# Products of keys and values on the whole array for batches 1 to 3, keys of a half copied to all 128 rows, with a new order of all instructions

## The chip, the cores and the metric

The kernel runs on one core of a Trainium2 chip. The metric is the device time of one execution in microseconds; the lower the better. Three executions of the kernel before took 168.55, 169.35 and 169.62 us (median 169.35). The profiled execution is the first of them: 168.55 us, of which 166.8 us lie between its first and its last instruction (the span), at a granted TensorE clock of 0.997.

In the profile, PE is TensorE's matmuls, PEld its weight loads, DVE is VectorE, ACT is ScalarE, POOL is GpSimd and SP is SyncE, which only issues DMAs here.

## The reference

A gated linear recurrence for 4 batches, 8 heads, 768 positions and 48 channels a head, and behind it an MLP mixer over tokens and channels:

```python
for t in range(S):                       # B, H, S, D = 4, 8, 768, 48
    state = alpha[:, :, t, :, None] * state + einsum('bhd,bhe->bhde', k[:, :, t], v[:, :, t])
    y[:, :, t] = einsum('bhd,bhde->bhe', q[:, :, t], state)
x = y.transpose(0, 2, 1, 3).reshape(B, S, 384)
h = maximum(x.transpose(0, 2, 1) @ w_tok1, 0) @ w_tok2      # 768 -> 256 -> 768
u = x + h.transpose(0, 2, 1)
out = u + maximum(u @ w_ch1, 0) @ w_ch2                     # 384 -> 1536 -> 384
```

## The kernel before

**Tiling.** Each batch is cut into three chunks of 256 positions; n = 3 * batch + chunk runs from 0 to 11. A chunk is loaded as one tile for each of q, k, v and alpha: 128 rows (partitions), two neighbouring positions ("slots", sl) in each row, 8 heads, 48 channels. Rows 0 to 63 hold the first half of the chunk (128 positions), rows 64 to 127 the second (hf = 0 and 1).

**Attention of a chunk.** `ln`, `P`, `lnP`, `cum`, `E`, `IE` make the running products of alpha and their inverses; `kk` and `qq` (L612) scale keys and queries by them into `pkk` and `pkq` in bf16, each head padded from 48 to 64 columns; for n >= 3, `k0a` and `q0r` scale one slot before. `vb` casts the values in place of rows, and `vs0_`, `vs1_` (`vswap`, L674) copy 64 rows of one slot to the other 64 rows, so that `vb[:, hf]` holds all 128 positions of half hf on 128 rows. Keys and queries are transposed on PE (`trk`, `trq`, copied by `evk`, `evq`) for n < 6, and by a transposing DMA on SP's queue (`dk`, `dq`, then the copy `pq`) for n >= 6. `G` makes the products of keys and queries of a half on 48-row, 64-column parts of the array, `mask` cuts them to the causal part, `y` multiplies them with the values, and `ia`, `ib` add the queries times the state. `x` copies the result out.

**State.** `K` (`kmm`, L678) makes the products of keys and values of each half: for each pair of heads j, slot, half and head r of the pair, one product of 64 rows, 64 columns of keys and 48 of values on a 64x64 quarter of the array, 32 of them where the chunk makes two states and 16 for the last chunk of a batch (nst = 1). The result has 192 columns, head r of a pair on rows 64 r. `s` or `sa` (L698, L702) read it twice over (`twice`), once for each head of the pair, and `s`/`sm` multiply by the decay with `amul`, whose factor is exp(-1024) = 0 for the block of the other head. So the state of a pair is a 128 x 96 matrix with two blocks that are zero.

**Mixer of a batch.** `t1`, `ht`, `t2`, `u` are the token MLP; `u` is transposed on PE for batch 0 (`up`, `ut`) and by a transposing DMA for the others (`ux`). `c1` (L765) and `rt` are the first channel layer in 24 groups of three 128x384 products, `c2` (L770) the second in 24 groups of three, `o` (L774) the last sum, `st` the store. `f1_` and `f3_` are one or three products of zeros that keep PE busy in the start; their results are overwritten.

**Order.** Nothing is scheduled at run time. `ORDER` lists every operation with a letter for its engine (t PE, s ACT, v DVE, g POOL, y SP), `BUFS` the buffer of each value; both were found outside the kernel with a planner's costs, which `build` still carries (`dve`, `act`, `pe` and so on) and which have no effect on what is emitted. Each engine works through its own operations in list order; waits come from the data. A DMA is issued by the queue of SP or ACT in its place in that list. One more wait is added by hand: an operation marked `port=True` that goes to DVE or POOL waits for the last marked operation on the other of the two (`shared`, L641), so that marked DVE and POOL operations never run at the same time:

```python
e, last = self.port_turn, self.port_last
if e:
    if last and last[0] != e:
        self.tc.add_manual_dep(i.ins, last[1].ins.name, ...)
    self.port_last = (e, i)
```

Marked are `P`, `k0a`, `q0r`, `kk`, `qq`, `vb`, `vs`, `sm`, `pq` and the casts of the weights (`cw_`).

Of the kernel before, what the change touches and what calls it, by code (L numbers as in the profile page):

```python
# [9 lines left out]
BF16 = mybir.dt.bfloat16  # L10
AF = mybir.ActivationFunctionType
ALU = mybir.AluOpType
# [51 lines left out]
class Plan:  # L64
# [32 lines left out]
NB = 3  # L97
NX = 6
OFF = -1024.0
# [5 lines left out]
    "la": 2, "lf": 2, "E": 2, "IE": 2, "pkq": 2, "pkk": 2, "vb": 3,  # L105
    "tpk": 4, "tpq": 2, "gtm": 2, "tmp": 2, "ss": 5, "x": 12, "ht": 3, "u": 4, "ut": 2, "rt": 22, "o": 3,
# [6 lines left out]
def build(g):  # L113
# [12 lines left out]
    def attention(n):  # L126
# [70 lines left out]
        for hf in range(2):  # L197
# [7 lines left out]
        KO = O("K", {"PE": (276.0 if nst == 2 else 140.0, 420.0)}, 9.5, writes=[kp], reads=[pkk, vb], preds=[kk, vc] + fill("K", kp) + ([prev_s[1]] if prev_s and k > 0 and n > NB else []),  # L205
               emit=lambda e: g.kmm(kp, pkk, vb, nst), mode="G")
        before = prev_s if k > 0 else None
        states = [before]
        for hf in range(nst):
            s_, sp = V("ss"), states[-1]  # L210
            if sp is None:
                so = O(f"s{hf}_", dve(384), 10, writes=[s_], reads=[kp, E], preds=[KO, et],
                       emit=lambda e, s_=s_, hf=hf: g.sfirst(s_, kp, E, hf, wide))
            else:
                t_ = V("tmp")
                ad = O(f"sa{hf}_", dve(384), 10 + hf, writes=[t_], reads=[kp, sp[0]], preds=[KO, sp[1]],
                       emit=lambda e, t_=t_, hf=hf, s0=sp[0]: g.sadd(t_, kp, s0, hf))
                so = O(f"sm{hf}_", either(dve(384), pool_tt(384)), 11 + hf, writes=[s_], reads=[t_, E], port=True,
                       preds=[ad, et], emit=lambda e, s_=s_, t_=t_, hf=hf: g.smul(e, s_, t_, E, hf, wide))
            states.append((s_, so))  # L220
        for hf, st in enumerate(states[:2]):
            yp, x = V("one"), V("x")
            vs = O(f"vs{hf}_", either(dve(384, True), act(384, True), {"POOL": (405.0, 440.0)}), 10, writes=[vb], reads=[vt],
                   port=True, preds=[KO, vc], emit=lambda e, hf=hf: g.vswap(e, vb, vt, hf))
            held = []
            if st:
                held.append(O(f"i{'ab'[hf]}", pe([96] * 4), 13, writes=[yp], reads=[tpq, st[0]], preds=[evq, st[1]],
                              emit=lambda e, hf=hf, st=st, yp=yp: g.inter(yp, tpq, st[0], hf)))
            yo = O(f"y{hf}_", pe([48] * 8), 14, writes=[yp], reads=[gtm, vb],
                   preds=[masks[hf], vs] + held + (fill("y", yp) if hf else []),  # L230
# [110 lines left out]
ld_kt0s ld_at0y ld_vt0s ld_at1y f1_trq0t ld_kt1s ld_qt0y f3_cumw1t ld_qt1y f1_K0t f1_cumw0t f3_cumw0t f1_cumw1t  # L341
f3_trk0t ln0s ld_at2y ld_vt1s cumw0t f3_K0t IE0s f3_trq0t ln1s kk0g ld_at3s ld_kt2y cumw1t E0s Et0s IE1s qq0v trk0t
ldw_wt10y E1s evk0s ld_qt2s Et1s kk1v trq0t ld_kt3y f3_cumw2t vb0v evq0v qq1g K0t f3_trq1t vs0_0s vb1s s0_0v f1_G00t
ld_qt3y G0_0t sa1_0v f1_trq1t f1_trk1t vs1_0g mask0_0v sm1_0g ld_vt2s K1t ln2s trq1t trk1t P3g sa0_1v evq1s f1_G10t
evk1v G1_0t sm0_1g cumw2t mask1_0v ln13s ldw_wt11y f3_G01t Et2s IE2s ld_at4y sa1_1v y0_0t f1_G01t lnP3s f1_y0t G0_1t
kk2v ib0t vs0_1s E2s mask0_1v sm1_1g f3_y1t f1_trk2t y1_0t f1_y1t r13s x0_0s vs1_1g f1_G11t ldw_wt20s x1_0s G1_1t qq2g
ib1t ld_vt3y mask1_1v ia1t cum3t y0_1t E3s trk2t ldw_wt21y vb2s x0_1v ld_qt4y cw_wt10g f1_trq2t evk2v f1_y2t y1_1t
IE3s trq2t k0a3v f1_K2t evq2s f3_K2t kk3v q0r3v t1_0_0_0t K2t t1_0_0_1t f1_G02t sa0_2v G0_2t t1_0_1_0t qq3g t1_0_0_2t
cw_wt11s ldw_wc14y mask0_2v f3_G12t f1_G12t ldw_wc15y vs0_2s x1_1s ldw_wc13y G1_2t P4g vs1_2s ldw_wc11y ld_at5y
t1_0_1_1t mask1_2v t1_0_1_2t ia2t ln14s ldw_wc10y y0_2t t1_0_1_3t trk3t r14s sm0_2v trq3t x0_2s vb3s evk3v t1_0_0_3t  # L350
ib2t y1_2t ldw_wc12y cw_wt21v x1_2s K3t lnP4s cw_wt20g t1_0_1_4t s0_3v t1_0_1_5t ld_kt4y t1_0_0_4t t1_0_0_5t ht_0_1s
cum4t sa1_3v ht_0_0s IE4s sm1_3v t2_0_3t ldw_wc23y vs0_3s t2_0_2t q0r4g u_0_3v E4s t2_0_5t t2_0_4t evq3s u_0_2v
ld_qt5y t2_0_1t cw_wc15g u_0_4v up_0_1t t2_0_0t u_0_5v cw_wc14s qq4g u_0_1v G0_3t u_0_0v ut_0_1s up_0_2t up_0_0t
ut_0_2v ld_kt5s cw_wc13g ut_0_0v trq4t ln15s mask0_3v cw_wc10g evq4s ld_at7y c1_0_10_1t c1_0_7_1t ldw_wc21y P5v
ldw_wc22y c1_0_8_0t cw_wc11v rt_0_7_1s cw_wc12s vs1_3s c1_0_6_1t c1_0_8_1t c1_0_10_0t rt_0_8_0s rt_0_10_1v lnP5s
c1_0_4_0t k0a4g rt_0_6_1v r15s c1_0_1_0t rt_0_10_0v ld_vt4y y0_3t rt_0_4_0v c1_0_0_1t kk4g ldw_wc20y x0_3s cum5t
ld_at6y rt_0_0_1v c1_0_1_1t E5s c1_0_5_1t IE5s rt_0_1_1v cw_wc23g c1_0_9_1t rt_0_1_0v c1_0_7_0t rt_0_8_1v c1_0_6_0t
rt_0_5_1v rt_0_7_0s c1_0_0_0t q0r5v k0a5v rt_0_6_0s G1_3t rt_0_9_1v qq5g c1_0_5_0t ldw_wc25y mask1_3v ldw_wc24y
c1_0_11_1t cw_wc21s ld_kt6y ld_qt6y c1_0_2_1t rt_0_0_0v rt_0_5_0s c1_0_3_0t rt_0_11_1v rt_0_2_1s c1_0_11_0t ld_vt5s
kk5v c1_0_4_1t rt_0_11_0s trq5t vb4s rt_0_3_0v c1_0_2_0t ld_vt6y P7v rt_0_4_1s ld_at9y trk5t rt_0_2_0s cw_wc20g  # L360
c1_0_3_1t evk5v K4t rt_0_3_1s trk4t sa0_4v cw_wc22s ib3t y1_3t c2_0_4_0t c2_0_1_0t sm0_4g vs0_4s x1_3v ln16s ld_qt7s
evk4v vs1_4s ln17s cw_wc25g c1_0_9_0t sa1_4v c2_0_4_1t rt_0_9_0s cw_wc24v G0_4t G1_4t P6g evq5s mask0_4v c2_0_4_2t
c2_0_1_1t sm1_4g c2_0_1_2t mask1_4v ld_kt7y c2_0_1_3t lnP6s ld_at8y k0a6g ld_vt7s c2_0_4_3t o_0_1v vb5s cum6t o_0_4v
ib4t c2_0_2_0t IE6s r17s K5t y1_4t c2_0_5_0t sa0_5v x1_4s G0_5t vs1_5s sm0_5g G1_5t ld_qt8y E6s mask0_5v c2_0_2_1t
# [463 lines left out]
```

## Time and profile before

| | value |
|---|---|
| runs, median | 168.55, 169.35, 169.62 us; 169.35 us |
| profiled execution, and its span | 168.55 us, 166.8 us |
| PE busy, share of span | 158.8 us, 95% |
| c1 (L765) and c2 (L770), 288 products each | 50.7 and 54.2 us |
| DVE, ACT, POOL busy | 118.5, 88.8, 63.9 us |
| read from HBM, written | 25.17 MB, 4.72 MB |
| a load of 384 KB, issue to landing | 4.4 to 10.0 us by kind (medians) |
| transposing DMA of keys, of u | 5.3 us, 3.0 us (medians) |

The DMA engines are busy for nine tenths and more of nearly every slice until 88 us, and for two tenths or less over most of the last 50 us. Times in the profile come from one execution. A matmul's duration in it includes the way through the array, some 0.16 us, which the next one overlaps; the step from one start to the next is what PE is held for.

### The profile page before, as it was taken

Reading aid. Unit: us, or ns where it says so; the run is one execution under the profiler, and the core shown is the slowest. Engines: PE = TensorE matmul, PEld = TensorE weight load, DVE = VectorE, ACT = ScalarE, POOL = GpSimd, SP = SyncE. Lnnn points to the kernel's source line nnn. Section 1 sums busy time; section 2 is a strip of 40 time slices with the busy share of each in tenths; the row PEclk is TensorE's granted clock in tenths of the full one; section 3 lists DMA queues with packets and bytes.
Section 4 is the critical chain, followed back from the end, with each engine's and each line's share of the span. In section 5 each row is a group of like instructions: output and inputs, shape, how many; then the busy total and the mean of one; then the engine's idle time right before and its main releaser. Section 6 shows DMA issues by size and latency. Waiting matters only on the chain.

```text
span 166.8 us, 4619 instructions
## 1 busy us (share of the span) xinstructions
PE 158.8 (95%) x1906; PEld 98.2 (59%) x1906; DVE 118.5 (71%) x208; ACT 88.8 (53%) x170; POOL 63.9 (38%) x68
## 2 busy tenths in 40 slices
PE   7969999889999999999899999999999999999991
PEld 2446565656566676565566676666566665665660
DVE  4059979889898869996998899892588463153522
ACT  3586978988678886735764842428602101641100
POOL 4139476296445661521646739436320000000000
PEclk9999999999999999999999999999999999999998
DMA  5999999999999999899999999489201186200213
GB/s 121 325 325 327 334 356 297 354 363 336 356 367 323 311 325 247 216 251 239 206 200 273 237 271 150 99 212 211 64 0 51 47 68 171 94 0 0 94 51 141
DMA packets 76757, 35.10 MB, mean 210 GB/s; under 512 B 70336, under 2 KB 75712, under 8 KB 76736
## 3 DMA queue, kind: packets, MB, share of 16 engines
q1 hardware_dynamic: 53168, 23.99, 58.5%
q10 hardware_dynamic: 23568, 10.82, 23.4%
q8 instruction: 15, 0.25, 0.7%
q14 instruction: 6, 0.05, 0.1%
HBM read 25.17 MB, written 4.72 MB: 179 GB/s over the span
## 4 chain that ended last, share of the span: by engine, by line
PE 76%; DMA 8%; DVE 6%; ACT 4%; issue 2%; SPq 1%; POOL 1%; DVEq 0%; ACTq 0%
PE ps L770 27%; PE ps L765 25%; PE ps L563 16%; DMA in<-in_q_dram 8%; PE ps L746 3%; PE ps L741 3%; PE ps L624 2%; DVE pkk L612 1%; ACT vb L654 1%; DVE o L774 1%; POOL tpq L655 1%; ACT tpq L654 1%; SPq L504 1%; DVE in L548 1%; DVE in L604 1%
## 5 line engine op out<-in xcount | busy, mean ns | idle before, releaser
L770 PE MATMUL ps<-wc,rt 128*128 128x384 bf16 x288 | 54.2, 326 | 0.1
L765 PE MATMUL ps<-ut,wc 128*128 128x384 bf16 x288 | 50.7, 326 | 0.7 <-DVE o L774 0.7
L736 ACT ACTIVATE rt<-ps 128x384 bf16<-128x384 f32 x52 | 23.5, 491 | 27.8 <-PE ps L765 27.6
L765 PEld LDWEIGHTS <-wc 128*128 128x128 bf16 x288 | 27.2, 98 | 18.4 <-issue 1.2
L770 PEld LDWEIGHTS <-rt 128*128 128x128 bf16 x288 | 26.7, 98 | 16.9 <-issue 0.3
L738 DVE TENSOR_SCALAR rt<-ps 128x384 bf16<-128x384 f32 x44 | 22.8, 551 | 15.5 <-PE ps L765 15.5
L670 DVE TENSOR_TENSOR gtm<-ps,mk 128x1024 bf16<-128x1024 f32 x24 | 28.8, 1220 | 3.6 <-PE ps L563 3.4
L774 DVE TENSOR_TENSOR o<-ps,u 128x384 f32<-128x384 f32 x24 | 13.1, 552 | 7.5 <-PE ps L770 7.4
L612 POOL TENSOR_TENSOR pkq<-in,E 128x768 bf16<-128x768 f32 x7 | 12.7, 1814 | 13.2 <-DVE in L608 7.1
L612 POOL TENSOR_TENSOR pkk<-in,IE 128x768 bf16<-128x768 f32 x7 | 12.7, 1814 | 10.7 <-ACT IE L596 5.2
L563 PE MATMUL ps<-zs 128*128 128x512 bf16 x51 | 15.5, 428 | 1.1 <-DVE zs L468 1.1
L654 ACT CAST vb<-in 64x384 bf16<-64x384 f32 (+1 forms) x24 | 14.5, 603 | 2.7 <-PE ps L563 2.0
L654 ACT CAST x<-ps 128x384 bf16<-128x384 f32 x18 | 8.3, 480 | 13.8 <-PE ps L563 12.6
L750 DVE TENSOR_TENSOR u<-ps,x 128x384 bf16<-128x384 f32 x24 | 12.4, 552 | 3.2 <-PE ps L746 3.1
L707 POOL TENSOR_TENSOR ss<-tmp,E 128x384 bf16<-128x384 f32 x10 | 8.4, 836 | 7.7 <-DVE vb L655 2.4
L703 DVE TENSOR_TENSOR tmp<-ps,ss 128x384 f32<-128x384 f32 x16 | 8.8, 552 | 1.9 <-PE ps L563 1.2
L746 PE MATMUL ps<-ht,wt 128*128 128x384 bf16 x48 | 9.8, 326 | 0.4 <-ACT ht L736 0.4
L612 DVE TENSOR_TENSOR pkq<-in,E 128x768 bf16<-128x768 f32 x5 | 4.8, 953 | 7.2 <-DMA in<-in_q_dram 7.1
L563 PEld LDWEIGHTS <-tpk 48*64 48x64 bf16 x384 | 6.3, 106 | 6.1 <-issue 4.9
L741 PE MATMUL ps<-x,wt 128*128 128x384 bf16 x48 | 9.6, 327 | 0.0
L563 PE MATMUL ps<-tpq,tpk 48*64 48x128 bf16 x384 | 9.1, 220 | 0.4 <-DVE u L750 0.2
L655 POOL COPY tpq<-tpk 128x1024 bf16<-128x1024 bf16 x5 | 6.7, 1339 | 5.8 <-PE ps L770 2.7
(85 smaller groups left out, 191.6 us busy)
## 6 DMA issues: line engine op xcount, KB each, us to landing
in<-in_moe_w_ch_dram SPq DMA_DIRECT2D x12, 384.0 KB, 6.4
in<-in_q_dram SPq DMA_DIRECT2D x10, 384.0 KB, 7.3
in<-in_alpha_dram SPq DMA_DIRECT2D x9, 384.0 KB, 6.5
in<-in_v_dram ACTq DMA_DIRECT2D x9, 384.0 KB, 6.3
in<-in_k_dram ACTq DMA_DIRECT2D x7, 384.0 KB, 5.8
out_dram<-o SPq DMA_DIRECT2D x13, 192.0 KB, 4.2
out_dram<-o ACTq DMA_DIRECT2D x11, 192.0 KB, 1.9
in<-in_k_dram SPq DMA_DIRECT2D x5, 384.0 KB, 6.9
```

Of the source, the lines that this page charges most:

```text
L563: return self.pe.matmul(out, lhsT=lhsT, rhs=rhs, start=start, stop=stop, skip_group_check=True)
L612: self.shared(self.eng[e].tensor_tensor(self.t(dst)[:, :, :, 0:D], self.t(src).rearrange("p h s d -> p s h d"), bass.AP(tensor=f.tensor, o ...
L654: return self.act.copy(d, s)
L670: self.nc.vector.tensor_tensor(self.t(gtm)[:, hf, :, :], self.pair(gp).rearrange("p a (j t) -> p (a j) t", t=128), bass.AP(tensor=m.tensor ...
L736: self.act.activation(d, s, AF.Relu)
L738: self.nc.vector.tensor_scalar_max(d, s, 0.0)
L741: self.pe.matmul(self.bank(bank)[:, 0:HD], lhsT=self.wt1[:, kc, m * 128 : m * 128 + 128], rhs=self.t(x), start=(kc == 0), stop=(kc == NS - 1))
L746: self.pe.matmul(self.bank(bank)[:, 0:HD], lhsT=self.wt2[:, kc, i * 128 : i * 128 + 128], rhs=self.t(hts[kc]), start=(kc == 0), stop=(kc = ...
L750: self.nc.vector.tensor_tensor(self.t(u)[:, i % 3], self.bank(bank)[:, 0:HD], self.t(x), ALU.add)
L765: self.pe.matmul(self.bank(bank)[:, 0:HD], lhsT=self.wc1[:, kc, mc * 128 : mc * 128 + 128], rhs=self.t(ut)[:, 3 * half : 3 * half + 3, kc, ...
L770: self.pe.matmul(self.bank(bank)[:, 0:HD], lhsT=self.t(rts[mc][0])[:, i * 128 : i * 128 + 128], rhs=self.wc2[:, mc, :], start=(mc == 0), s ...
L774: self.nc.vector.tensor_tensor(self.t(o), self.bank(bank)[:, 0:HD], self.t(u)[:, i % 3], ALU.add)
```

## The change

For n >= 3 (`KFN = 3`) `K` is made in another way; for batch 0 it stays as it was.

- `kc` copies the keys of slot 1 of rows 0 to 63 onto rows 64 to 127 of slot 0 in `pkk`, so that `pkk[:, 0]` holds the 128 positions of the first half on 128 rows. Before it, where two states are made (nst = 2), `ka` and `kb` copy rows 64 to 127 of both slots into a new tile `kt`, which then holds the second half. `kc` waits for the transposition of the keys (`trk`, or the landing of `dk`), since it writes over them, and for `ka`.
- `kfull` multiplies 128 rows, 128 columns of keys (two heads) and 96 of values: four products a half, eight or four a chunk. It reads `vb` after `vs`; before, `vs` waited for `K`.
- The result has 384 columns and holds the blocks of the other head too; `sfirst` and `sadd` read it as it is (`kparts`), and the zeros of `amul` still take those blocks away.
- `ka`, `kb`, `kc` may run on DVE, ACT or POOL and are marked for the shared port. In the new order the 21 of them are 12 on ACT, 7 on POOL, 2 on DVE.
- Buffers: E 2 to 3, pkk 2 to 3, ss 5 to 4, kt 1, x 12 to 9, rt 22 to 20.
- `ORDER` and `BUFS` are replaced as a whole: other places, other engines for many operations, other queues for many loads.

The core of the diff:

```diff
+KFN = 3
...
+        vsw = lambda hf, preds: shift(f"vs{hf}_", 10, [vb], [vt], preds, lambda e: g.vswap(e, vb, vt, hf))
+        turned = n >= KFN
+        if turned:
+            vs = [vsw(hf, [vc]) for hf in range(2)]
+            kx, kp_in = None, [kk, vc, vs[0]]
+            if nst == 2:
+                kx = V("kt")
+                ka = shift("ka", 9, [kx], [pkk], [kk], lambda e: g.kturn(e, kx, pkk, 0))
+                kb = shift("kb", 9, [kx], [pkk], [kk], lambda e: g.kturn(e, kx, pkk, 1))
+                kp_in += [ka, kb, vs[1]]
+            kc = shift("kc", 9, [pkk], [], [kk, trk if n < NX else evk] + ([ka] if nst == 2 else []),
+                       lambda e: g.kturn(e, None, pkk, 2))
+            KO = O("K", pe([96] * (4 * nst)), 9.5, writes=[kp], reads=[pkk, vb] + ([kx] if kx else []),
+                   preds=kp_in + [kc] + ([prev_s[1]] if prev_s and k > 0 and n > NB else []),
+                   emit=lambda e: g.kfull(kp, pkk, kx, vb, nst))
...
+    def kturn(self, e, kx, pkk, part):
+        k = self.t(pkk)
+        d, s = ((self.t(kx)[0:64] if kx else None, k[64:128, 0]), (self.t(kx)[64:128] if kx else None, k[64:128, 1]),
+                (k[64:128, 0], k[0:64, 1]))[part]
+        self.copy(e, d[:, :, 0:D], s[:, :, 0:D])
+
+    def kfull(self, kp, pkk, kx, vb, nst):
+        vv = self.t(vb)
+        for hf in range(nst):
+            kk = self.t(kx) if hf else self.t(pkk)[:, 0]
+            for j in range(4):
+                self.mm(self.bank(kp, hf)[:, 96 * j : 96 * j + 96], kk[:, 2 * j : 2 * j + 2, :],
+                        vv[:, hf, 2 * j : 2 * j + 2, :], j == 0, j == 3)
...
+    def kparts(self, kp, hf, turned):
+        b = self.bank(kp, hf)
+        return self.st(b[:, 0:HD]) if turned else self.twice(b[:, 0:192])
```

The new order around the places that matter for batch 1 and 2 (engine letters at the end of each name):

```diff
+ORDER = """
+ld_qt0s ld_at0y ld_kt0s ld_at1y f1_trk0t ld_kt1s ld_vt0y f1_cumw0t f1_cumw1t f1_trq2t f1_trq1t f3_cumw0t ld_vt1y ln0s
+ld_qt1y f3_trq0t f3_cumw1t ld_at2s cumw0t f3_trk0t IE0s f1_trq0t ld_kt2y f3_trq2t Et0s ln1s kk0v E0s cumw1t qq0v trk0t
...
+c2_0_0_0t x0_5s qq6v c2_0_0_1t ln18s k0a6v x1_5s IE7s c2_0_0_2t c2_0_2_2t E7s P9v t1_1_0t IE6s ld_qt8s kk6v c2_0_0_3t
+vb7s t1_1_1t o_0_0v dk6y r18s ht_1_0v vs1_7g c2_0_3_0t c2_0_2_3t kk7g o_0_1v ht_1_1s lnP9s t2_1_3t ld_kt9s t2_1_4t
+ka6s u_1_3v t2_1_5t P11g c2_0_3_1t u_1_4v t2_1_0t u_1_5v cum9t vs1_6g u_1_0v ux_1_1y c2_0_5_0t k0a8g o_0_2v c2_0_5_1t
+t2_1_1t q0r8g st_0_0y t2_1_2t u_1_1v kc6s c2_0_3_2t st_0_1y u_1_2v kb6s vs0_6g c2_0_3_3t ln19s ux_1_0y vb8v c2_0_5_2t
+IE9s P8v K6t lnP11s c2_0_5_3t k0a9v E9s dk7y s0_6v lnP8s kk9g c1_1_0_1t ka7s sa1_6v c1_1_10_1t vs0_7s o_0_3v dq6y
+rt_1_0_1s c1_1_8_1t rt_1_10_1v ld_qt9s c1_1_6_1t sm1_6v kb7s c1_1_2_1t c1_1_3_1t vs1_8s o_0_5v rt_1_8_1s q0r7g r19s
+c1_1_7_1t rt_1_6_1v qq7g rt_1_3_1s c1_1_11_1t rt_1_2_1v rt_1_7_1s cum8t ld_at10y c1_1_1_1t IE8s c1_1_4_1t E8s kc7g
+dq7y c1_1_10_0t rt_1_11_1s kk8g rt_1_1_1s c1_1_5_1t rt_1_4_1s K7t rt_1_10_0s rt_1_5_1v ld_vt9y sa0_7v c1_1_5_0t sm0_7v
...
+"""
```

## The prediction

> **What bounds the kernel now.** I read the page's busy times and 40 slices first, then who waited for whom on PE, then the chain of waits, then PE's timeline stage by stage, then the groups by shape for the price of one instruction.
>
> ```profile
> PE 158.8 (95%) x1906; PEld 98.2 (59%) x1906; DVE 118.5 (71%) x208; ACT 88.8 (53%) x170; POOL 63.9 (38%) x68
> ...
> PE   7969999889999999999899999999999999999991
> ...
> DVE  4059979889898869996998899892588463153522
> ```
>
> PE is full in nearly every slice; DVE stands at 8 or 9 tenths up to about 100 us and falls off after. The next view is PE's waits (total us, times, longest):
>
> ```profile
> PE ps L563 <- DVE zs L468: 1.1, 1, 1.1
> PE ps L624 <- DVE pkq L612: 0.8, 1, 0.8
> PE ps L765 <- DVE o L774: 0.7, 1, 0.7
> PE ps L563 <- ACT vb L654: 0.4, 1, 0.4
> PE ps L746 <- ACT ht L736: 0.4, 1, 0.4
> ```
>
> After 38 us only the 0.7 is left. The chain of waits gives the two marks I work with:
>
> ```profile
> 37.88 4.06 PE ps L765 x24
> ...
> 158.03 5.38 PE ps L770 x33
> 163.41 0.02 issue
> 163.43 0.56 DVE o L774
> ```
>
> From the first channel product (c1, L765) at 37.88 to 163.4 PE is the path; before it the path runs through loads, DVE, ACT and POOL; after it 3.4 us go to the last sum and store. So the span is a start of 37.9, PE's work of 125.5, and 3.4: 166.8. The profiled run took 168.55, 1.75 more, and is the fastest of three with median 169.35, so I scale by 1.0047 at the end.
>
> **The products of keys and values on PE.** PE's timeline (start, us, what):
>
> ```profile
> 50.44 0.65 PE L765 MATMUL ps<-ut,wc 128*128 128x384 bf16 x3
> 51.02 0.44 PE L563 MATMUL ps<-vb,pkk 64*64 64x48 bf16 x32
> 51.39 0.62 PE L624 MATMUL ps<-idn,pkk 128*128 128x128 bf16 x8
> ...
> 95.54 0.42 PE L563 MATMUL ps<-tpq,tpk 48*64 48x128 bf16 x16
> 95.79 0.42 PE L563 MATMUL ps<-vb,pkk 64*64 64x48 bf16 x32
> 96.04 0.43 PE L563 MATMUL ps<-tpq,tpk 48*64 48x128 bf16 x16
> ```
>
> Three L765 products take 0.49, so they give PE free at 50.93; the group K4 holds it until 51.39: 0.46. Between score products (G), which also use part of the array, K9 takes 95.79 to 96.04: 0.25. Coming from and going back to the whole array thus costs about 0.2 a time. The new products have the shape of the state products, 128x96 on the whole array: eight of them start at 61.90 and the next instruction at 62.24, so 0.34 for eight, 0.17 for four. In batches 1 to 3 that is 6 x 0.34 + 3 x 0.17 = 2.55, against 9 x 0.25 = 2.25 plus the switches. In the old order there are 25 stretches of part-array work, 14 of them after the first c1; in the new one 21 and 11.
>
> The Trainium skill (TensorEngine Tiling (Array Packing), When to Use Tiling) says that a contraction or a free dimension of 64 and less is where splitting the array pays; by this alone the change would lose 0.3 us, 2.55 against 2.25, and the row inside G bears it out. The Trainium skill (same page, Key Properties) also says that a change of mode drains the array; the trace agrees, with the 0.2 of a K group by itself.
>
> After the first c1 I add up both orders with the steps of this timeline (c1 and c2 groups 0.49, t1 0.98, t2 0.33, G 0.25, y 0.20, state products 0.17, cum 0.29): old 121.4 + 14 x 0.2 = 124.2, so the old 125.5 hold 1.3 of standing; new 121.0 + 11 x 0.2 = 123.2. The first terms fall by 0.4: the K groups of n = 4 to 11 give 2.21 in the place of 2.0, and two groups move ahead of the first c1 (cum5 0.29, G1_3 0.25). The rest is three stretches fewer, 0.6. **PE after the mark: -1.0.** Ahead of it the order has 54 warming products (L563, 512 wide, 0.21 warm) in the place of 51: 0.6, at nothing, because PE waits there for the other engines anyway; without that cover it is 0.6.
>
> **The copies.** 21 come in: kc 9, ka 6, kb 6. The trace has no bf16 to bf16 copy of 64x384; the nearest rows are the casts of that size:
>
> ```profile
> L654 ACT CAST vb<-in 64x384 bf16<-64x384 f32 x17 | 8.7, 510 | 2.7 <-PE ps L563 2.0 <-issue 0.4
> ...
> L655 POOL CAST vb<-in 64x384 bf16<-64x384 f32 x5 | 2.5, 501 | 7.2 <-DVE ss L707 4.0 <-DVE in L604 3.0
> ...
> L655 DVE CAST vb<-in 64x384 bf16<-64x384 f32 x2 | 0.7, 356 | 0.1
> ```
>
> 12 on ACT are 6.1 us, 7 on POOL 3.5, 2 on DVE 0.7; I take these, with half of them as the lower bound and the 128x768 casts (0.83 on ACT and POOL, 0.55 on DVE) as the upper. The Trainium skill (VectorE: DVE Perf Modes, Mode 4x_2P) lets a copy between two 16-bit tiles in SBUF run at four elements a cycle; an estimate from it is 0.1 us plus a fixed part for each of the two DVE copies, 0.4 less on DVE and nothing in the sum, and no run here shows it. ACT has 27.6 us of waiting for c1 alone in this trace and hides its share; on POOL the copies stand in the chain of the shared port.
>
> **The new order on the other engines.** I count the instructions of both order lists by engine and multiply by the mean durations in the groups by shape. POOL gets kk 7 to 10, qq 7 to 9, k0a 4 to 6, q0r 3 to 6, vs 5 to 9, loses weight casts 8 to 5: 63.0 to 77.6 us. DVE 127.0 to 122.8 in durations (118.5 busy, since neighbours overlap by a tenth), ACT 97.9 to 103.8. The marked DVE and POOL instructions wait for each other in order: this chain grows from 88.1 to 96.7 us, over some 115 us, from 8 to 123. It isn't full, and I price it only in the start and where PE waits for it (below). Before, the half copies of v (vs) waited for K, which read v in place; now K waits for them, and they may go ahead of it. The buffers cut for the new tiles (x 12 to 9, rt 22 to 20, ss 5 to 4) I take at nothing: six x of a batch are read by u (68 to 71 us in batch 1) before the next batch writes its first (90), and the c2 of a batch are nearly done when c1 of the next begins (73.7); if a writer did wait, one c2 group, 0.5, is what it waits for.
>
> **The start.** Old: DVE first waits for q until 10.19, t2 starts at 32.65, first c1 at 37.88. New: q and k of n = 0 are the first loads on ACT, kk0 goes to DVE at 7.9 (where POOL began it before), qq0 at 9.5, vb0 ends at 10.9. Then the shared chain binds, by steps of the timelines (POOL 1.76 for kk and qq, 0.95 for 384 wide, 0.79 for sm, 0.78 for casts, 0.48 for halves; DVE 0.47, 0.87 for 768, 1.13 for masks): kk1, vb1, qq1 to 15.4; sm1_0 16.0; kk2 17.9; sm0_1, vs1_0, P3 to 19.8; sa1_1 and qq2 21.1; sm1_1, k0a3, kk3 24.8; P4, cw_wt21, q0r3 26.3. Now DVE binds: sa0_2, two masks to 29.0, x0_2, x0_1, vb3, x1_2 to 30.9. The last t1 products end at 31.3, K3 and ht bring t2 at 32.3, six sums u run to 36.0, two ut copies to 37.1; on POOL qq4 and the casts of wc14 and wc15 end at 37.2. First c1 at 37.4: -0.5. Bounds: DVE has 31.5 instead of 27.9 queued ahead of the first c1 (3.3 with the overlap), starts 2.3 sooner, so 38.9 if it has no slack; ACT has 1.7 less queued, so 36.3.
>
> **Standing after the mark.** The 0.73 at 79.2 goes: DVE stood for a q load there (q0r9) that SP sent late; q0r7 to q0r9 now run on POOL and ACT sends q7 to q9. What is late next is K6. It stands in PE's queue between c2 groups and now needs vs0_6 and kc6. vs0_6 is on POOL behind kk7, P11, vs1_6, k0a8, q0r8, and q0r8 needs a q load (7.3 us to landing); PE has 8.6 us of work listed from that load to K6 (nine c2 groups, two t1, six t2, cum9), against 7.3 + 1.0 + 0.5 + 0.1: 0.3 late. kc6 waits, on ACT, for the transposing DMA that still reads these keys:
>
> ```profile
> tpk<-pkk SPq DMA_TRANSPOSE x6, 5.3
> ```
>
> 7.1 us of PE's work against 5.3 + 0.5 + 0.1: in time; with the longest landing of that tile, 6.2, too. kb6, ln19, IE9 and lnP11 queue behind kc6 on ACT. K7 after kc7 on POOL (kk8 behind it): 6.2 of work against 5.9, or 6.8 at the longest: 0 to 0.6. The first c1 of batch 1 has 3.9 us behind the transposing DMA of u, which takes 3.0 to 4.8: 0 to 0.9. I take 0.9 for the three, so 1.3 - 0.73 + 0.9 = 1.5; bounds 0.6 and 4.
>
> **Sum:** 37.4 + 123.2 + 1.5 + 3.4 = 165.5 span, 167.25 for this run, 168.0 by the median: 0.8% faster.
>
> **The rivals.** *Faster by over 1%*: start at the lower bound, no new standing: 36.3 + 123.2 + 0.6 + 3.4 = 163.5, 166.0 by the median. For it: DVE is relieved up to 100 us. Against: the shared chain fills the start. *Slower*: K6 waits for the q load behind POOL's queue. If that load lands after 10.0 us (the slowest kind in the page, a weight) instead of 7.3, K6 is 3.0 late, and K7, behind the same POOL queue, 1.5 more; with the start at 38.9: 38.9 + 123.2 + 5.1 + 3.4 = 170.6, 173.2 by the median. It decides above some 4.5 us of standing in all, delay of the start included. For it: DMA is 9 tenths busy until 88 us. Against: ACT sends the load unblocked. *It does not do what it says*: three of nine K groups lay inside G, where only 0.25 could be saved; if the other six switch as often as before, 0.6 goes and the result is 168.6, no change.
>
> **Numbers.** About 1% is what a measurement of this kernel tells from no change: 167.7 to 171.0. Forecast, with the third rival, 0.37; faster 0.34; slower 0.29. The range 165.8 to 172.2 leaves out the ends of both rivals; the likeliest case alone is 167.0 to 169.5.
>
> **What would show it.** 128x96 products of vb in the place of 64x48, 0.34 for eight; the first L765 near 37.4; no wait for o before L765; PE waits before the K groups n = 6 and 7 under 1 us in sum. A PE wait there of 2 us or more, or a first c1 after 39, makes me wrong.

## The result, and the profile after

The changed kernel takes 169.28 us (median of 20 runs, 168.96 to 171.6). The kernel before, run 20 times too, takes 169.2 us (167.48 to 170.81). The ratio of after to before, which leaves out runs more than 1.5% above the fastest of their kernel, is 1.0053, with a 95% interval of 1.0031 to 1.0076: slower by 0.3 to 0.8%, inside the 1% that the prediction takes as no change. The medians of all 20 differ by 0.05%. The forecast was 168.0, faster by 0.8%.

From the page of the changed kernel, busy times and slices:

```profile
PE 158.8 (95%) x1729; PEld 98.9 (59%) x1729; DVE 115.4 (69%) x205; ACT 95.2 (57%) x180; POOL 78.5 (47%) x84
...
PE   7898997989999999999999999999999999999991
...
DVE  4096989999797997878477998887287161663232
...
POOL 4037565798839720958898976884200000000000
```

PE is busy for the same 158.8 us with 177 products fewer in the trace. POOL has 14.6 us more (77.6 were worked out), DVE 3.1 less. PE's thin place behind the first slices is the seventh, 25.1 to 29.3 us; before it had 9 there. PE's waits (total us, times, longest):

```profile
PE ps L588 <- ACT la L582: 1.4, 3, 0.8
PE ps L588 <- DVE zs L491: 1.1, 1, 1.1
PE ps L588 <- DVE tmp L745: 0.9, 1, 0.9
PE ps L787 <- ACT ht L777: 0.4, 1, 0.4
PE ps L782 <- ACT wt L679: 0.3, 1, 0.3
PE ps L588 <- POOL pkk L680: 0.2, 1, 0.2
...
```

The first five are in the start; the wait for o at 79.2 is gone, and the last one shown (before K7) is the only one listed after the first c1. The chain of waits (start, us, what) gives the marks; c1 is L806 now, c2 L811, t1 L782:

```profile
5.76 8.65 DMA in<-in_q_dram
14.57 1.82 POOL pkq L637
17.11 1.83 POOL pkk L637
...
32.24 1.32 PE ps L782 x8
35.31 1.03 DVE u L791 x2
39.43 3.52 PE ps L806 x21
...
154.97 8.79 PE ps L811 x54
163.75 0.02 issue
163.78 0.56 DVE o L815
```

The first c1 starts at 39.36 (the chain's piece begins where the product before it ends, at 39.43), PE ends at 163.74, the span is 167.2. So start, PE's part and tail are 39.36 + 124.4 + 3.4, against 37.88 + 125.5 + 3.4 before and 37.4 + 124.7 + 3.4 in the forecast (123.2 and the 1.5 of standing taken together). The start grew by 1.5; it was to fall by 0.5. PE's part fell by 1.1, where 0.8 was forecast. Here it is by itself, before and after (from:to, length, us; busy us of PE, PEld, DVE, ACT, POOL; granted clock; DMA):

```profile
37.88:163.40 125.52, 124.59 (x1398) 77.99 (x1398) 91.24 (x155) 60.67 (x124) 43.16 (x39) 1.00 0.77 182
39.36:163.74 124.38, 124.05 (x1227) 77.81 (x1220) 84.98 (x144) 67.42 (x135) 55.54 (x53) 1.00 0.73 179
```

PE was busy for 0.5 less and stood for 0.3 in the place of 0.9.

The K groups in PE's timeline (start, us, what), n = 4:

```profile
50.19 0.61 PE L649 MATMUL ps<-idn,pkk 128*128 128x128 bf16 x8
50.63 0.33 PE L588 MATMUL ps<-vb,pkk 128*128 128x96 bf16 x4
50.80 0.33 PE L588 MATMUL ps<-vb,kt 128*128 128x96 bf16 x4
50.97 1.25 PE L806 MATMUL ps<-ut,wc 128*128 128x384 bf16 x6
```

From 50.63 to 50.97 are 0.34 for eight products, and c1 follows at once: nothing of the 0.2 at each side is left. The new copies, by shape (count, busy us, mean ns, idle before):

```profile
L680 DVE COPY pkk<-pkk 64x384 bf16<-64x384 bf16 x2 | 0.5, 253 | 0.1
L679 ACT COPY kt<-pkk 64x384 bf16<-64x384 bf16 x10 | 5.1, 509 | 0.5 <-POOL pkk L637 0.3
L679 ACT COPY pkk<-pkk 64x384 bf16<-64x384 bf16 x2 | 1.0, 509 | 1.0 <-DMA tpk<-pkk 0.9
L680 POOL COPY pkk<-pkk 64x384 bf16<-64x384 bf16 x5 | 2.5, 498 | 0.3
L680 POOL COPY kt<-pkk 64x384 bf16<-64x384 bf16 x2 | 1.0, 500 | 0.1
```

They cost what the casts of that size cost on ACT and POOL, and 253 ns in the place of 356 on DVE. The Trainium skill (VectorE: DVE Perf Modes, Mode 4x_2P) states four elements a cycle for two ports with two packed bf16 each; that the copy is faster than the cast agrees with it, and the rate itself no run here shows.

### The profile page after: what moved, and what is told of

Read it like the earlier page. It is cut to its first block, busy times and chain, and to the rows that moved or that the text cites. A ratio compares the mean times of both kernels' runs of the same rounds, so it can differ in the third digit from the quotient of the medians.

```text
span 167.2 us, 4293 instructions
## 1 busy us (share of the span) xinstructions
PE 158.8 (95%) x1729; PEld 98.9 (59%) x1729; DVE 115.4 (69%) x205; ACT 95.2 (57%) x180; POOL 78.5 (47%) x84
## 4 chain that ended last, share of the span: by engine, by line
PE 76%; DMA 5%; POOL 5%; DVE 4%; ACT 4%; SPq 3%; issue 1%; POOLq 0%; DVEq 0%
PE ps L811 28%; PE ps L806 25%; PE ps L588 11%; DMA in<-in_q_dram 5%; PE ps L782 5%; PE ps L787 4%; SPq L529 3%; POOL pkk L637 2%; POOL pkq L637 2%; PE ps L649 1%; ACT vb L679 1%; ACT tpq L679 1%; DVE ss L748 1%; PE ps L798 1%; DVE gtm L695 1%
## 5 line engine op out<-in xcount | busy, mean ns | idle before, releaser
L811 PE MATMUL ps<-wc,rt 128*128 128x384 bf16 x288 | 53.0, 326 | 0.0
L806 PE MATMUL ps<-ut,wc 128*128 128x384 bf16 x288 | 50.4, 326 | 0.1
L777 ACT ACTIVATE rt<-ps 128x384 bf16<-128x384 f32 x54 | 24.6, 492 | 26.9 <-PE ps L806 26.7
L806 PEld LDWEIGHTS <-wc 128*128 128x128 bf16 x288 | 27.4, 98 | 17.9 <-issue 0.5
L811 PEld LDWEIGHTS <-rt 128*128 128x128 bf16 x288 | 27.0, 98 | 17.0 <-issue 0.2
L779 DVE TENSOR_SCALAR rt<-ps 128x384 bf16<-128x384 f32 x42 | 22.1, 553 | 14.3 <-PE ps L806 14.0
L637 POOL TENSOR_TENSOR pkk<-in,IE 128x768 bf16<-128x768 f32 x10 | 18.2, 1817 | 12.9 <-DVE vb L680 8.5
L637 POOL TENSOR_TENSOR pkq<-in,E 128x768 bf16<-128x768 f32 x9 | 16.3, 1818 | 3.8 <-DVE in L633 1.7
L680 POOL CAST vb<-in 64x384 bf16<-64x384 f32 (+1 forms) x12 | 7.0, 582 | 11.4 <-ACT lf L585 4.9
L679 ACT CAST vb<-in 64x384 bf16<-64x384 f32 (+1 forms) x19 | 11.3, 597 | 0.4
L679 ACT CAST x<-ps 128x384 bf16<-128x384 f32 x13 | 6.1, 479 | 8.7 <-PE ps L588 8.4
L782 PE MATMUL ps<-x,wt 128*128 128x384 bf16 x48 | 9.3, 326 | 0.3 <-ACT wt L679 0.3
L748 POOL TENSOR_TENSOR ss<-tmp,E 128x384 bf16<-128x384 f32 x9 | 7.5, 836 | 3.9 <-DVE pkq L637 2.2
L588 PEld LDWEIGHTS <-zs 128*128 128x128 bf16 x54 | 5.1, 103 | 5.8 <-issue 1.9
```

The source lines that it names most:

```text
L588: return self.pe.matmul(out, lhsT=lhsT, rhs=rhs, start=start, stop=stop, skip_group_check=True)
L637: self.shared(self.eng[e].tensor_tensor(self.t(dst)[:, :, :, 0:D], self.t(src).rearrange("p h s d -> p s h d"), bass.AP(tensor=f.tensor, o ...
L679: return self.act.copy(d, s)
L777: self.act.activation(d, s, AF.Relu)
L779: self.nc.vector.tensor_scalar_max(d, s, 0.0)
L782: self.pe.matmul(self.bank(bank)[:, 0:HD], lhsT=self.wt1[:, kc, m * 128 : m * 128 + 128], rhs=self.t(x), start=(kc == 0), stop=(kc == NS - 1))
```

## The experiments

They ask two things: whether the gain on PE comes from the products, and what holds the start. In the diffs the letters behind a name are the engine; order lists are cut to the places that change. PE's part is always first c1 to PE's end.

### The products

**Old K in the new order.** vs goes back behind K, as the old products need it.

```diff
-KFN = 3
+KFN = 12
...
-ib3t ka4s y1_3t ... rt_0_8_1s kb4s x1_3s ... c1_0_5_1t kc4v vs1_4s ... vs0_4g r15s
+ib3t y1_3t ... rt_0_8_1s x1_3s ... c1_0_5_1t ... r15s ... K4t vs1_4s vs0_4g
...
```

> The new order with the old products of keys and values everywhere (KFN = 12): the 21 copies are gone, vs stands behind K. If the new products are worth on PE what the timelines say (after the first c1 five groups of 0.46 for 0.34 and three of 0.46 for 0.17): PE's part from the first c1 is 1.5 longer than 124.4. Theory A: the first c1 is 1.0 to 1.5 earlier than 39.36 as the copies leave ACT; the span is then within 0.5 of 167.2. Theory L: the first c1 stays near 39.2 and the span is 168.4 to 168.7. Rival for the products (the copies cost as much after the mark as the products save): PE's part stays at 124.4.

174.94 us, ratio 1.0322 (1.0268 to 1.0375). PE's part is 127.9, 3.5 more, of which 2.3 are waits:

```profile
PE ps L805 <- DVE tmp L744: 0.9, 1, 0.9
PE ps L587 <- ACT vb L678: 0.6, 1, 0.6
PE ps L587 <- ACT x L678: 0.5, 1, 0.5
PE ps L805 <- DMA ut<-u: 0.3, 1, 0.3
```

PE is busy for 125.52 of these 127.9, 1.5 more than in after: that is the groups themselves with their switches, as expected. The other 2.1 are standing, and they are the larger share; only the wait for vb is by its row a wait for vs, which stands behind K here, and that the others follow from it isn't shown. The Trainium skill (TensorEngine Tiling (Array Packing), When to Use Tiling) gives a contraction or a free dimension of 64 and less as the case for splitting the array. Inside other part-array work a group of small products is the cheaper one in this kernel, too, 0.25 (K9 of before) against 0.34 (K4 of after); between products on the whole array, at 0.46 (K4 of before), it is not. First c1 is at 42.0: the clock fell to half from 29.7 to 33.1 (below), so nothing is read from this start.

**The old start, then the new order.** All of the list of before up to the first c1, then that of after; buffers are assigned anew where the two lists meet.

```diff
-ld_qt0s ld_at0y ld_kt0s ... t1_0_0_0t ... G1_3t ut_0_2s
+ld_kt0s ld_at0y ld_vt0s ... t1_0_0_0t ... trq4t evq4s
 c1_0_10_0t ...
```

> The order of the kernel before up to its first c1, then the order of the changed kernel for all that is left; n = 3 the old way, n = 4 to 11 the new way. If the start alone is what the change loses and the rest what it gains: first c1 at 37.9, from there to PE's end 124.4 as in the changed kernel plus 0.5 for two groups that the changed kernel had made before its first c1, span 166.2 to 166.4: 0.5% under the changed kernel and 0.3% under the kernel before. Rival (the rest is short only because its start left more vector work done): PE's part grows to 125.5 or more and the span is 167 or more.

171.31 us, 1.0143 (1.01 to 1.0185). First c1 38.76, PE's part 128.4: 2.8 of waits in it (1.1 for rt, 1.0 for E, 0.7 for the q copy), and from the first c1 to the first c2 17.5 in the place of 13.6. The old start leaves work undone that the new one has behind it, five operations of n = 3 and 5 among it (G1_3, cum5, lnP5, E5, IE5). So the rival came true: PE's part of the new order is short only behind the new start. How much of this comes from the reassigned buffers isn't told apart.

**The old order with the new products alone**, n = 4 to 6 and 8 to 11:

```diff
-        turned = n >= KFN
+        turned = n in (4, 5, 6, 8, 9, 10, 11)
...
-K4t trk4t sa0_4v ... sm0_4g vs0_4s x1_3v evk4v vs1_4s
+kb4s ka4s vs0_4s ... vs1_4s ... trk4t kc4s ... K4t sa0_4v ... sm0_4g x1_3v evk4v
...
```

> The order of before in every stage, with one part of the change alone: n = 4, 5, 6, 8, 9, 10 and 11 make K from 128x96 products and copies (ka, kb on ACT, kc on ACT or POOL); their vs stand ahead of K, K itself up to 4 us of PE work later where kc has to wait for the transposition; n = 3 and 7 as before. The start is that of before, so first c1 at 37.9. Theory P (the products themselves are worth what was worked out, 0.1 to 0.3 for a group that stands alone, nothing inside G): PE's part from there 124.8 in the place of 125.5, span 166.1, ratio 0.996. Rival W (the added wait for vs and kc takes the gain back): PE waits before a K group of over 0.5 in sum, span 166.8 or more, ratio 1.000 to 1.005.

175.07 us, 1.037 (1.0322 to 1.0418). First c1 37.6 as in before, PE's part 132.3. PE's waits from there:

```profile
PE ps L785 <- DVE tmp L743: 1.1, 1, 1.1
PE ps L586 <- DVE tmp L743: 1.1, 2, 0.6
PE ps L647 <- ACT rt L775: 1.0, 1, 1.0
PE ps L586 <- DVE o L813: 1.0, 1, 1.0
...
```

Theory P falls, and W as well as it was put: only 0.2 of waiting stands directly before a K group. But ka, kb and vs of n = 4 lie together on ACT from 49.75 to 51.3, and the rt behind them stops PE for 1.0 at 51.9; after that DVE is late again and again up to 131 us. The added copies and waits do take the gain back, through the queues of ACT and DVE and at many times the price. It shows this placing of the copies, put in by hand, not that none would do.

So the new products save PE work, and in these runs the saving reached the time of PE's part only with the new order from the first instruction on. In the changed kernel and the fourteen experiments with its order after the first c1 that follow, PE's part stays between 124.4 and 124.8 whatever the start does. The total moves with the first c1 alone.

### The start: loads

The walk in the prediction against the trace of after: kk2 17.9 at its end, measured 18.9; sa0_2 26.3, measured 27.5; masks of n = 2 done 29.0, 30.3; x1_2 done 30.9, 32.6; t2 32.3, 34.4; first c1 37.4, 39.36. One microsecond is lost by kk2, and one more in steps from there to t2.

**The q load of n = 1 ahead of v.** POOL's qq1 stood for it until 14.57, and DVE 1.30 behind that.

```diff
-f3_cumw0t ld_vt1y ln0s ld_qt1y f3_trq0t
+f3_cumw0t ld_qt1y ld_vt1y ln0s f3_trq0t
...
-s0_0v vb1g f1_G00t ... vs0_0s mask0_0v
+s0_0v f1_G00t ... vs0_0s vb1s mask0_0v
```

> The changed kernel with the load of q for n = 1 sent before that of v for n = 1 on SP's queue, and the cast of that v (vb1) taken from POOL to ACT, where there is a gap after vs0_0. Theory L (the start is late because POOL's qq1 stood for its load until 14.57 us and the shared chain of DVE and POOL carried that delay): qq1 starts at about 13.0, kk2 0.6 to 0.7 earlier than 17.11, the first c1 0.7 earlier (38.7 instead of 39.36), the span 166.5. Theory A (ACT's queue sets the end of the start): the first c1 stays within 0.2 of 39.36.

169.58 us, 1.0034 (1.0002 to 1.0067); first c1 39.50. qq1 began at 13.32, but then the next loads came last, first k of n = 2 (kk2 stood 1.97 until 17.10), then its q. The first c1 came no sooner, as theory A had it. The chain:

```profile
13.07 8.18 DMA in<-in_q_dram
21.25 0.02 issue
21.27 0.96 DVE pkq L637
```

One load alone is not it: all of them are on their way at once, at 325 GB/s, and what is brought forward pushes back its neighbour. A run below (f5_dve_clock) shows by accident what a late load does. There the k load of n = 2 took 9.88:

```profile
8.01 9.88 DMA in<-in_k_dram
...
18.05 1.81 POOL pkk L645
```

kk2 began 0.94 later than in after, ACT's cast of wt10 0.84 later, and the first c1 0.85 later (40.21).

### The start: one engine at a time

**The copies of n = 3 gone** (old K for n = 3: 1.0 us off ACT, 0.5 off POOL).

```diff
-KFN = 3
+KFN = 4
...
-t1_0_1_0t kb3s trq3t x0_1v ka3g lnP4s ... cum4t vs1_3g kc3s x1_2v ... vs0_3s
+t1_0_1_0t trq3t x0_1v lnP4s ... cum4t x1_2v ... E4s vs0_3s ... qq4g vs1_3g
```

> The changed kernel with n = 3 made the old way (KFN = 4): the three copies ka3, kb3, kc3 are gone and vs0_3, vs1_3 stand behind K3. On ACT that takes 1.0 us of copies and 0.5 of vs0_3 from ahead of ht. Theory A (ACT's queue sets the end of the start, and the copies of the change are a part of it): t2 and the first c1 1.0 to 1.5 earlier, span 165.7 to 166.2. Theory L (the late load and the shared chain): the first c1 earlier by 0.3 at most, span 167.0 or more.

170.13 us, 1.0049 (1.0014 to 1.0084); first c1 39.33, the same. The copies alone do not hold the start.

**ACT's queue reordered:** vs0_2 and the cast of wt10 ahead of evk3, cum4 and IE4 behind t1.

```diff
-evk3s ... vs0_2s G1_2t ia2t cw_wt10s ... vb3v cw_wt11s ... cum4t ... IE4s ... ht_0_0s
+vs0_2s cw_wt10s G0_2t ... evk3s ... cw_wt11s kb3s ... cum4t K3t ... ht_0_0s IE4s
```

> The changed kernel with ACT's queue put in another order between 26.7 and 34 us: vs0_2 and the cast of the first token weight (cw_wt10) ahead of evk3, cw_wt11 ahead of kb3, and cum4 and IE4 behind the t1 products and ht. Theory Q (the start is late because the t1 products stand behind ACT's cast at 30.07 and PE then works off 2.0 us of queue before the last eight of them): t1 starts at 29.3 to 29.5, t2 0.4 to 0.8 earlier than 34.39, the first c1 at 38.6 to 39.0. Theory D (DVE's queue sets the end of the start, by the masks that end at 30.2): t2 within 0.2 of 34.39.

170.4 us, 1.0081 (1.004 to 1.0122). In the profiled run the first t1 product began at 30.21, no sooner than in after: it now waits 0.38 for evk3, whose PSUM bank it takes. t2 and the first c1 (39.12) came 0.24 earlier, between what Q and D expected. The clock averaged 0.99 in 8 of its 12 runs, 168.5 to 169.3 of span against 166.8 to 167.4 in the other four, so the median is one with the lower clock.

**DVE's queue reordered** (G0_1 ahead of y1_1; P4 and the cast of wt21 behind vb3 and x1_2), **both**, and **both with u's way shortened** (ut_0_0 on ACT, sa1_3 behind u):

```diff
-evk2v y1_1t ... G0_1t ... P4v trk3t cw_wt21v ... vb3v cw_wt11s ... x1_2v
+evk2v G0_1t y1_1t ... trk3t ... vb3v P4v lnP4s cw_wt11s ... x1_2v cw_wt21v
```

> The changed kernel with DVE's queue relieved between 23 and 31 us: P4 and the cast cw_wt21 go behind vb3 and x1_2, and PE makes G0_1 ahead of y1_1, so that mask0_1 needn't wait 0.64. Theory D: the last mask of n = 2 ends at 28.7 instead of 30.2, t2 1.0 to 1.6 earlier than 34.39. Theory Q: the t1 products still wait for ACT's cast at 30.07, t2 within 0.3 of 34.39.

> Both edits. If the start is held by both queues together: t2 at 32.6 to 33.0, the first c1 at 37.7 to 38.2, the span 165.7 to 166.3, so 0.3 to 0.6% under the kernel before. Rival L (the loads hold the start, whatever the queues do): first c1 above 39.

> Both edits, and the first copy of the transposed u (ut_0_0) on ACT, with sa1_3 behind the six sums u on DVE: 0.5 to 0.8 less on DVE between t2 and the first c1. If DVE's queue holds that last stage: first c1 at 37.0 to 37.6, span 165.2 to 165.8, 0.6 to 1.0% under the kernel before. Rival (POOL's casts of wc14 and wc15, which end at 38.37 in the changed kernel, hold it): first c1 at 38.0 or later, no better than with the two edits alone.

171.38, 170.52 and 171.05 us (1.0187, 1.0134 and 1.0163, all above 1.008 at the lower end); first c1 41.6, 40.6 and 42.7. None shows the gain it was made for; the rivals of the second and third (first c1 above 39; at 38.0 or later) come true by the number, but not by their cause. G0_1 shares its banks with trk2, so PE waited 0.6 to 0.9 there for evk2 and 0.57 more behind it for x; in the first it then waited 1.1 for vb, in the other two 0.9 for evk3. How much of the later c1 each wait makes isn't told apart. In the third the clock fell, too.

**Work taken off one engine, every queue as it was.** Some operations are done for one head of eight, and the rest of them is left out: P4, q0r3, vb3 on DVE; vb2, vs1_2, vs0_2 on ACT; vs1_0, k0a3 on POOL.

```diff
+CUT = ["P4", "q0r3", "vb3"]
...
-        a = self.t(at)
+        a = self.t(at)[:, 0 : self.heads]
...
+            g.heads = 1 if o.name in CUT else 8
             o.emit(o.on)
```

> The changed kernel with three operations of the start that run on DVE ahead of the last t1 products (P4, q0r3, vb3) done for one head of eight: some 1.3 us less work on DVE, every queue as it was. It leaves out part of these products and of one cast. Theory D (DVE is the path of the start: 28 us of work between 8.7 and 39.1 with 2.5 of gaps): first c1 1.0 to 1.3 earlier, 38.0 to 38.4. Theory A (ACT's queue paces it): 0 to 0.3 earlier. Theory L (the loads pace it): 0 to 0.3 earlier, DVE standing longer instead.

> The changed kernel with three casts of the start that run on ACT (vb2, vs1_2, vs0_2) done for one head of eight: some 1.2 us less work on ACT between 24.6 and 29.2. It leaves out the rest of these casts. Theory A: t1 products begin 0.8 to 1.2 earlier and first c1 too, 38.2 to 38.6. Theories D and L: first c1 within 0.3 of 39.36, though t1 begins earlier.

> The changed kernel with two operations of the start that run on POOL in the shared chain (vs1_0, k0a3) done for one head of eight: some 1.2 us less on POOL. It leaves out the rest of them. Theory S (POOL's share of the shared chain holds DVE up): first c1 0.6 to 1.2 earlier. Theories A, D and L: within 0.3 of 39.36.

First c1 40.79, 39.10 and 39.35. POOL is out (theory S falls), ACT gives 0.26 of 1.2 taken away (theory A falls). With less work on DVE it came 1.4 later, with the granted clock at half for a time (from:to, length, us; busy us of PE, PEld, DVE, ACT, POOL; granted clock; DMA):

```profile
28.00:29.00 1.00, 0.66 (x21) 0.51 (x21) 1.00 (x2) 0.99 (x3) 1.00 (x2) 1.00 1.15 370
29.00:30.00 1.00, 0.48 (x13) 0.48 (x13) 0.86 (x1) 0.98 (x2) 0.94 (x3) 0.74 1.10 341
30.00:31.00 1.00, 0.94 (x11) 0.47 (x9) 0.96 (x3) 0.95 (x3) 0.39 (x1) 0.50 1.12 345
31.00:32.00 1.00, 1.00 (x10) 1.00 (x9) 0.17 (x2) 1.00 (x2) 0.68 (x2) 0.50 1.08 398
```

The granted clock, ahead of the last two numbers, is 0.50 from 29.4 to 32.8. So the run says nothing of DVE. It was made again with three warming products into a free bank ahead of y0_2, to keep PE from standing:

```diff
+            if o.name == "y0_2":
+                g.fill2(2, 3)
             o.emit(o.on)
```

> f1_dve_less again (P4, q0r3 and vb3 for one head of eight, the rest of them left out), with three more warming products ahead of the y product that waits from 28.65 to 29.52, so that PE does not stand there and its granted clock should stay at 1.0 (in f1_dve_less it was 0.50 from 29.4 to 32.8). Theory D (DVE is the path of the start): first c1 at 38.0 to 38.4. Theory Q (from the first t1 product on, PE's own queue is the path, so less work on DVE gains nothing): first c1 39.0 to 39.5. If the clock falls again, no verdict on either.

The clock stayed. With the k load 0.94 late, the first t1 product and the first c1 (40.21) are both 0.85 late: of the 1 us taken off DVE 0.1 came through at most in this execution. DVE stood 1.22 for PE ahead of x1_2 instead, and the first t1 product still waited 0.30 for ACT's cast. Theory D falls, as far as one execution with a late load can tell. The same on PE, eight of the twelve t1 products 96 columns wide:

```diff
+        w = 96 if self.early and 0 < kc < NS - 1 else HD
-        self.pe.matmul(self.bank(bank)[:, 0:HD], ..., rhs=self.t(x),
+        self.pe.matmul(self.bank(bank)[:, 0:w], ..., rhs=self.t(x)[:, 0:w],
```

> The changed kernel with eight of the twelve t1 products of batch 0 made 96 columns wide in the place of 384: some 0.8 us less work for PE between 30.1 and 33.6, every queue as it was. It leaves out the rest of these products. Theory Q: first c1 0.5 to 0.8 earlier, 38.6 to 38.9. Theory D: within 0.2 of 39.36. If the clock falls, no verdict.

First c1 40.36, with the clock at 0.50 from 29.4 to 32.8: no verdict on PE.

### The start: several queues together

In after, PE has this before t2 (timeline, start, us, what, the wait before it):

```profile
29.25 0.56 PE L588 MATMUL ps<-vb,gtm 128*128 128x48 bf16 x16 [0.17 <-ACT vb L679]
30.11 0.50 PE L782 MATMUL ps<-x,wt 128*128 128x384 bf16 x2 [0.30 <-ACT wt L679]
...
32.10 1.46 PE L782 MATMUL ps<-x,wt 128*128 128x384 bf16 x8
...
34.39 1.78 PE L787 MATMUL ps<-ht,wt 128*128 128x384 bf16 x10 [0.40 <-ACT ht L777]
```

All twelve t1 products come after 30.11, when the last mask is nearly done. In before the first ran at 24.89, and when its last mask of n = 2 was done, at 29.33, these five were left:

```profile
29.75 0.33 PE L741 MATMUL ps<-x,wt 128*128 128x384 bf16 x1
31.20 0.82 PE L741 MATMUL ps<-x,wt 128*128 128x384 bf16 x4
```

PE works off a queue after that the walk did not have.

**PE's queue mended:**

```diff
-ldw_wt20y ... ldw_wt10y ... cw_wt20s ... trk3t cw_wt21v ... cw_wt10s
+ldw_wt10y ... ldw_wt20y ... cw_wt10s ... trk3t y0_1t t1_0_0_0t cw_wt21v ... cw_wt20s
...
-y0_2t ... y0_1t x0_2v t1_0_0_0t ... t1_0_1_0t ... trq3t x0_1v t1_0_0_1t f1_y2t vb3v ib2t y1_2t ... x1_2v
+y0_2t t1_0_0_1t t1_0_1_0t ... ib2t y1_2t ... x0_1v x0_2v ... trq3t ... x1_2v vb3v
```

> The whole computation, in the order of the changed kernel with PE's queue of the start mended: the loads and casts of wt10 and wt20 change places, y0_1 and the first t1 product go into the 0.91 us in which PE stands at 27.2 (that t1 group gets another PSUM bank), ib2 and y1_2 go ahead of trq3, x1_2 ahead of vb3, one warming product goes. Theory Q: PE has 0.7 us less to work off from 30.1 on and x1_2 is there 0.5 earlier, so first c1 at 38.5 to 38.9, span 166.3 to 166.7, ratio to before about 1.000. Theory D (DVE's queue ahead of c1 has the same work): first c1 39.1 to 39.4, ratio 1.004.

169.51 us, 1.0044 (1.0009 to 1.0078); first c1 39.36, not a tenth earlier, though the first t1 product ran at 26.85 and x1_2 was done at 31.7. ACT's timeline says where it went:

```profile
32.40 0.49 ACT L618 ACTIVATE IE<-ps 128x384 f32<-128x384 f32 x1
32.92 0.51 ACT L679 CAST vb<-in 64x384 bf16<-64x384 f32 x1
33.45 0.87 ACT L777 ACTIVATE ht<-ps 128x384 bf16<-128x384 f32 x2
```

ACT is busy for 11.84 of the 12.30 between 22.0 and 34.3, and ht, which t2 needs, comes when its turn is there. Theory Q falls as it was put: PE's queue was not the path alone; PE's t1 ended at 33.22 and ACT's queue ahead of ht at 33.43. By the numbers theory D comes true here; the next run tells it from ACT's queue.

**ACT's queue as well:** the step of the old K for n = 3, which had gained nothing by itself, cum4, IE4 and vs0_3 behind ht, wt11 before wt20.

```diff
-cw_wt20s ... kb3s ... lnP4s ... cw_wt11s ... kc3s ... IE4s ... vs0_3s ... ht_0_1s ht_0_0s E4s
+cw_wt11s ... lnP4s cw_wt20s ... K3t cum4t ht_0_1s ht_0_0s IE4s E4s vs0_3s
```

> The whole computation: g1_pe_queue with ACT's queue relieved as well. n = 3 makes K in the old way (no ka3, kb3, kc3), cum4, IE4 and vs0_3 go behind the two ht, the load and cast of wt11 change places with those of wt20. Theory J (the start is paced by PE's and ACT's queues together: g1 had PE done with t1 at 33.2 and ACT without a gap from 22.0 until ht at 33.45): ht at 32.7, t2 at 33.6, first c1 at 38.5 to 38.8, span 166.4 to 166.7, ratio to before 0.997 to 1.000. Rival (DVE's chain of masks, x and the q copy sets it): t2 at 34.2 or later, first c1 39.1 or later, ratio 1.003 or more.

168.94 us, 1.0042 (1.0007 to 1.0077); t2 33.71, as theory J expected, first c1 38.98, between J's 38.8 and the rival's 39.1. So DVE's chain of masks did not hold t2. Now DVE had no gap from 25.1 on, and the sums u began when it was free.

**And DVE's:**

```diff
-trk3t y0_1t t1_0_0_0t cw_wt21v vs1_2s ... cw_wt20s ldw_wc10y
+trk3t y0_1t t1_0_0_0t vs1_2s ... cw_wt20s cw_wt21s ldw_wc10y
```

> The whole computation: g2_start with one more step, the cast of wt21 taken off DVE (it stood ahead of sa0_2) and put on ACT behind the cast of wt20, where ACT stood for 1.48. In g2_start DVE ran without a gap from 25.1 to beyond the first c1. Theory B (the start is three queues nearly level, and after PE and ACT were relieved DVE's is the longest): everything behind sa0_2 comes 0.4 to 0.5 earlier, t2 at 33.2 to 33.4, first c1 at 38.4 to 38.7, span 166.3 to 166.6, ratio to before 0.996 to 1.000. Rival (the first c1 is held by something that these queues do not show, since two mended queues gave only 0.38 so far): first c1 38.9 or later, ratio 1.002 or more.

168.45 us against 168.62 of before beside it: ratio 0.9994 (0.9967 to 1.0022). Theory B: t2 33.30, first c1 38.57, PE's part as ever:

```profile
33.30 1.79 PE L787 MATMUL ps<-ht,wt 128*128 128x384 bf16 x10
...
38.57 1.64 PE L806 MATMUL ps<-ut,wc 128*128 128x384 bf16 x9
```

1 us off DVE alone had gained 0.1 at most; with PE and ACT out of the way, 0.47 is worth 0.41. POOL's cast of wc15 ends at 38.7, and the first c1 group needs it in its third product, so the next step would meet a fourth queue. This version is level with before; the loss is undone, and a gain is not shown. The marks of each step come from one execution; by the ratios to before (1.0053 for after, then 1.0044, 1.0042, 0.9994) only the three steps together are clear of the noise.

## Why the prediction failed

**What held.** The marks: 39.36 + 124.4 + 3.4 is the span. The K group of eight at 0.34, no switch left, so the third rival falls. The copies on ACT and POOL, and POOL's total. The wait at 79.2 gone. For the new waits 0.9 was taken and 0.21 came: K6 started at 73.37 without one, K7 waited 0.21 at 81.07 (0 to 0.6 was the bound), the first c1 of batch 1 none, at 74.20. The slower rival, K6 behind POOL's queue, did not happen. The buffers cut at nothing show no wait on PE.

PE's part came nearer than its terms: -1.1 for -0.8. PE's busy time there fell by 0.5 where 1.0 was taken, and its standing fell from 0.9 to 0.3 where it was to grow from 1.3 to 1.5. That the two errors partly cancel is luck.

**The step that failed is the start, 37.4 by the walk, in the place of 39.36**; it was the term itself, and its upper bound of 38.9 was too low as well. The first c1 after 39 is a sign that the prediction names for being wrong, and with 39.36 its own sum gives a span of 167.5, where 167.2 was measured. Three parts of it, with what the runs showed:

- The loads. The walk has qq1 begin at 13.6 and kk2 end at 17.9. The q load of qq1 landed at 14.41, POOL stood 0.77 for it, and kk2 ended at 18.94. Mending this one load moved the wait to the next (e1_q_first), and a load 0.94 late made the first c1 0.85 late, although DVE had less to do in that run (f5_dve_clock).
- "Now DVE binds" was the choice from 26.3 on, with PE and ACT walked past. sa0_2 was 1.2 late by then and the masks 1.3; for x1_2, 1.7 late, DVE had to stand 0.32 for PE; the last t1 product ended at 33.56 for 31.3, 2.3 late, and t2 was 2.1 late. PE had all twelve t1 products to work off behind ACT's cast at 30.1, and ACT a queue up to ht. Relieving DVE alone gained 0.1 at most, POOL alone 0, ACT alone 0.26, PE's order alone 0; PE and ACT together 0.38, with DVE 0.79.
- The bound of 38.9 let DVE start 2.3 sooner than before, 7.9 against 10.19; it started at 8.73, 1.46 sooner. Up to the last ut copy DVE was then busy for 27.6 us against 24.8 before, with 2.8 us of gaps in each: 2.8 - 1.46 = 1.4 of the 1.5 by which the start grew. The working had 3.3 for the 2.8; with the true start of DVE it would have given 39.7. This adds the growth up on DVE; that DVE alone did not set it, f5_dve_clock and the step of g2_start show.

The warming products were taken at nothing, since PE waits there anyway. The working doesn't ask whether they keep PE busy enough: from 26.0 to 29.4 it was busy for all of 3.40 us before and for 2.31 after. In the profiled execution of after the clock stayed at 1.00 there; in executions of four variants with the new start it fell (last section).

What stays open: PE's share by a cut of its own (the clock fell), how much of the first microsecond the loads make by themselves, and how the old start would do with its own buffers kept. The gains above are read from one execution of each kernel.

## What to carry to other kernels

When a change brings a new order, its start is a piece of work of its own: walk every queue up to the mark, PE's with the products that wait for the last input and ACT's with what stands ahead of each hand-over, not only the engine that looks fullest. Where cutting any one engine gains nothing, look for several level queues before looking for a hidden cause: relieve them one after another and keep the steps that gained nothing. A gain on a full PE can count only behind the point from which PE is the path, and there, too, only where the engines that make its operands have room: in e11_old_order the added copies cost PE's part 6.8 us.

## What the runs showed of the hardware

The granted clock fell to 0.50 for 3.4 us although PE never stood for long: in f1_dve_less and f4_pe_less from 29.4 to 32.8, in e6_old_k from 29.7 to 33.1, in e10_all from 31.4 to 34.8. In the 3.4 us before, PE was busy for 2.43, 2.34, 2.31 and 2.10 of 3.40, and its longest stand was 0.9. After's profiled run had 2.31 of 3.40 in 26.0 to 29.4 and kept its clock; up to 29.4 f4_pe_less has the very same queues. So the same queues can meet a fall in one execution and none in another. The Trainium skill (TensorE: Matmul & The Clock Gate, Why this matters for your kernels) warns of PE gaps above some 3 us; here the clock fell with no stand longer than 0.9, and the measurement decides. The Trainium skill (same page, Part 1) states a free-running window of 3.4 us, with which the length of the fall agrees; that this window is the cause, no run here shows.

What sets the chance of a fall stays open. A granted clock of 0.99 over a whole run was shown by 4 of the 20 runs of after, three of them with spans of 168.8 to 169.0 and one with 169.9, against 167.2 to 168.6 in the others. The busy time from 26.0 to 29.4 doesn't order it: e7_act, with 2.53, shows 0.99 in 8 of 12 runs, g1_pe_queue and g2_start, with 2.67, in 1 of 10 and 2 of 12, g3_wt21_act, with 2.67, in none of 12.
